# Cutting the first load of w2 in two, and moving the gate's sum between the halves

## The chip, the cores and the metric

The kernel runs on one core of a Trainium2 chip. The metric is the time of one execution on the device in microseconds (us). A second source is the hardware profile of one execution, with the start and length of every instruction. All data is float32.

## The reference

The reference is one decode step of a transformer block for 4 sequences with one token each (model width 512): an attention over the last 2048 entries of a key/value cache with 32 query and 8 key/value heads, and a gated MLP with inner width 1792. Both are conditioned by a vector c: silu(c) times w_mod gives six vectors per sequence, a shift, a scale and a gate for each half.

```python
mod = (_silu(c) @ w_mod).reshape(c.shape[0], 6, 1, -1)
sa, ca, ga, sb, cb, gb = (mod[:, 0], ..., mod[:, 5])
h = _layernorm(x) * (1 + ca) + sa
x = x + ga * attention(h)                # wq, 2048 cached keys and values, softmax, wo
h = _layernorm(x) * (1 + cb) + sb
hidden = _silu(h @ w1) * (h @ w3)        # 512 -> 1792
x = x + gb * (hidden @ w2)               # 1792 -> 512
```

The change concerns the last line alone: the product with w2, and the gate gb.

## The kernel before, in words

One instance of everything: there is no outer loop over data, and the instructions of each engine are written out in order. What one engine needs of another is awaited with semaphores. All large loads are issued by SyncE (SP) through the helper `load` at line 89, on one queue and in the order in which they are used: the conditioning weights, then keys, values and attention weights for the eight head groups, then w_mod's middle part, w1 and w3, the gate's part of w_mod (`gb_in`, 1 MB), and last w2. A load goes out when the buffer it overwrites is free; the last ten or so are all issued long before their data is used, and from then on they follow one another on the queue.

TensorE works through the attention in a loop over pairs of head groups (block "pair"), and then goes on in the straight code of block "post". Matrix products go through the helper `mm` (line 266), transposes through `turn` (line 287). The batch has only 4 rows, so a product here has 4 columns of weights loaded, and four products that write to partitions 0, 32, 64 and 96 of the same PSUM tile are placed side by side.

The end of block "post", which the change touches, goes like this:

- `hidT` is the hidden vector, transposed, in 14 chunks of 128 (lines 424 to 440; line 440 writes the last of it). w2 has 1792 rows, so 14 chunks of 128 rows by 512 columns, 256 KB each. `CHUNKS` is the order in which they are loaded and used.
- The gate: four products of silu(c) with the gate's weights go to the four quarters of tile `bM` (line 445). ScalarE copies them to `gb_sb` (448). A product with `same`, a matrix of zeros and ones, adds the four quarters and lays the sum out as four blocks of 128 columns at partitions 0, 32, 64 and 96 of tile `bT` (line 462); ScalarE copies that to `gbJ` (465). This is "the gate's sum".
- w2's first `HEAD` = 8 chunks: chunk n multiplies its 512 columns into quarter n % 4 of tile `bO` (line 456). VectorE copies `bO` to `y_sb` (459), and four products with `same` add the four quarters into tile `bX`, in the same layout as the gate's sum (475). This is "the sum of y".
- The last 6 chunks go into `bX` directly, each in four column blocks of 128 (line 471), so nothing needs to be summed behind them.
- VectorE multiplies `bX` by `gbJ` (478) and adds the residual `x1J` (480), and SP stores the result (482).

`W2_CUTS` says how w2's 14 chunks are cut into loads. Each load has its own semaphore, `dw[i]`, on which TensorE waits before it multiplies that piece.

Of the kernel before, what the change touches and what calls it, by code (L numbers as in the profile page):

```python
# [10 lines left out]
B, D, HQ, G, SK, DH, W, FF = 4, 512, 32, 8, 8192, 128, 2048, 1792  # L11
P = 128
# [2 lines left out]
EPS = 1e-5  # L15
CHUNKS = [(j, c) for c in range(4) for j in range(4) if c < 2 or j < 3]
HEAD = 8
W2_CUTS = [0, 8, 10, 12, 13, 14]
PAIRS = G // 2


# [22 lines left out]
def block_kernel(nc, x_in, t0_in, t1_in, kv_in, w_in, wm_in, f1_in, f2_in, gb_in, w2_in, out):  # L44
    T, v, s, gp, S = nc.tensor, nc.vector, nc.scalar, nc.gpsimd, nc.sync

    def sems(names):
        return [nc.alloc_semaphore(n) for n in names.split()]

    def sb(name, cols, rows=P):  # L50
        return nc.alloc_sbuf_tensor(name, (rows, cols), F32).ap()

    def bank(name):
        return nc.alloc_psum_tensor(name, (P, 512), F32).ap()

    (first,) = sems("first")
    A = Queue(nc, s, "act")
    V = Queue(nc, v, "dve")
    L = Queue(nc, gp, "pool")
    dx, dt0, dt1, dkv, dk, dva, dvb, dwo, dm, df1, df2a, df2b, dgb = sems("dx dt0 dt1 dkv dk dva dvb dwo dm df1 df2a df2b dgb")  # L60
    dw = sems(" ".join(f"dw{i}" for i in range(len(W2_CUTS) - 1)))
    z_ok, q_ok, p_ok, k_ok, va_ok, vb_ok, pt_ok, o_ok, ot_ok = sems("z_ok q_ok p_ok k_ok va_ok vb_ok pt_ok o_ok ot_ok")
    s_done, q_done, qt_done, pp_done, o_done, x_done, a_done, pe, last = sems("s_done q_done qt_done pp_done o_done x_done a_done pe last")
# [6 lines left out]
    ident, same, eps = sb("ident", P), sb("same", B), sb("eps", 1)  # L70
# [3 lines left out]
    q_sb, p_sb, o_sb, a_sb, y_sb, g_sb, u_sb, gb_sb = [sb(n, 512) for n in "q_sb p_sb o_sb a_sb y_sb g_sb u_sb gb_sb".split()]  # L74
# [7 lines left out]
    x1J, gbJ, yt, y = [sb(n, P) for n in "x1J gbJ yt y".split()]  # L82
    zero = y_sb

    bS, bQ, bT, bP, bO, bX, bA, bM = [bank(n) for n in "bS bQ bT bP bO bX bA bM".split()]


    def load(dst, src, sem):
        S.dma_start(dst, src).then_inc(sem, 16)  # L89
# [33 lines left out]
    load(KV[1][:, 6144:8192], gb_in, dgb)  # L123
    for a, b, sem in zip(W2_CUTS[:-1], W2_CUTS[1:], dw):
        load(KV[1][:, 8192 + a * 512 : 8192 + b * 512], w2_in[:, a * 512 : b * 512], sem)
# [139 lines left out]
    def mm(o, lhsT, rhs, start=True, stop=True):  # L265
        return T.matmul(o, lhsT, rhs, start=start, stop=stop, skip_group_check=True)  # L266
# [46 lines left out]
    for k in range(4):  # L313
        for i in range(2):
            ins = mm(bM[32 * i : 32 * i + B, :], sc[:, k * B : (k + 1) * B], T0[:, 16 + (2 * k + i) * 512 : 16 + (2 * k + i + 1) * 512], k == 0, k == 3)
    ins.then_inc(pe, 1)
    T.wait_ge(V.sem, t_h[1])
    for k in range(4):
        ins = T.transpose(bT[:, k * B : (k + 1) * B], h[:, k * P : (k + 1) * P], ident[:B, :B])
# [51 lines left out]
    for k in range(4):  # L371
        for i in range(3):
            at = (3 * k + i) * 512
            ins = mm(bX[32 * i : 32 * i + B, :], sc[:, k * B : (k + 1) * B], KV[0][:, at : at + 512], k == 0, k == 3)
# [19 lines left out]
    for k in range(4):  # L394
        ins = T.transpose(bT[:, k * B : (k + 1) * B], h[:, k * P : (k + 1) * P], ident[:B, :B])
# [4 lines left out]
    def view(t_):  # L400
        return t_.rearrange("p (c j i) -> p c j i", c=4, j=4)
# [4 lines left out]
    for k in range(4):  # L406
        for j in range(4):
            at = 6144 + k * 2048 + j * 512
            ins = mm(bQ[32 * j : 32 * j + B, :], h2T[:, k * B : (k + 1) * B], KV[0][:, at : at + 512], k == 0, k == 3)
# [3 lines left out]
    for k in range(4):  # L413
# [5 lines left out]
        for j in range(3):  # L419
            at = k * 1536 + j * 512  # L420
            ins = mm(bA[32 * j : 32 * j + B, :], h2T[:, k * B : (k + 1) * B], KV[1][:, at : at + 512], k == 0, k == 3)
# [14 lines left out]
    for c in range(4):  # L436
        ins = T.transpose(bS[:, c * P : c * P + 96], u_sb[:96, c * P : (c + 1) * P], ident[:96, :96])
# [6 lines left out]
    for k in range(4):  # L444
        ins = mm(bM[32 * k : 32 * k + B, :], sc[:, k * B : (k + 1) * B], KV[1][:, 6144 + 512 * k : 6144 + 512 * (k + 1)])
    ins.then_inc(pe, 1)
    A.wait((pe, 10))
    t_gb = A.op(s.copy(gb_sb, bM))
    T.wait_ge(V.sem, t_hid[1])
    hw = view(hidT)  # L450
    w2 = KV[1][:, 8192 : 8192 + 14 * 512].rearrange("p (n m) -> p n m", n=14)
    T.wait_ge(dw[0], 16)
    for n in range(HEAD):
        j, c = CHUNKS[n]
        i = n % 4
        ins = mm(bO[32 * i : 32 * i + B, :], hw[:, c, j, :], w2[:, n, :], n < 4, n >= HEAD - 4)
    ins.then_inc(pe, 1)
    V.wait((pe, 11))
    t_y = V.op(v.tensor_copy(y_sb, bO))
    T.wait_ge(A.sem, t_gb[1])  # L460
    for j in range(4):
        ins = mm(bT[32 * j : 32 * j + B, :P], same, gb_sb[:, j * P : (j + 1) * P])
    ins.then_inc(pe, 1)
    A.wait((pe, 12))
    t_gb = A.op(s.copy(gbJ, bT[:, :P]))
    for i in range(1, len(W2_CUTS) - 1):
        T.wait_ge(dw[i], 16)
        for n in range(W2_CUTS[i], W2_CUTS[i + 1]):
            jj, c = CHUNKS[n]
            for j in range(4):  # L470
                ins = mm(bX[32 * j : 32 * j + B, :P], hw[:, c, jj, :], w2[:, n, j * P : (j + 1) * P], n == HEAD, n == 13)
        if i == 1:
            T.wait_ge(V.sem, t_y[1])
            for j in range(4):
                mm(bX[32 * j : 32 * j + B, :P], same, y_sb[:, j * P : (j + 1) * P], False, False)
# [56 lines left out]
```

## Time and profile before

| | us |
|---|---|
| median of 3 runs | 244.55 |
| lowest and highest of them | 243.27, 245.59 |
| the profiled execution | 245.33 |
| its span, first to last instruction | 244.0 |
| DMA queue of SP, share of the span in which its packets moved | 96.9% |
| TensorE busy, share of the span | 57% |
| mean granted clock of TensorE | 0.811 |

How to read the profile: times are us from the start of the span. PE is TensorE, PEld its weight loads, DVE VectorE, ACT ScalarE, SP SyncE. An instruction is named by its line, the tile it writes and the tiles it reads (`bO<-KV,hidT`); the buffers `KV0` and `KV1` are both called KV. Each `mm` shows as two instructions on PE. The granted clock is 1.00 where TensorE runs at full speed and 0.50 where it runs at half. For a load, "to landing" counts from its issue to the moment when its data is complete; loads of w2 are listed as `KV<-w_in`, with the other loads by the names of their sources. A view in windows gives, for each stretch of time, the busy time of each engine with the count of instructions.

### The profile page before, as it was taken

How to read it: one execution, taken by the hardware profiler on the slowest of the kernel's cores; microseconds unless marked ns; L12 is line 12 of the kernel's file. 1: busy time of each engine (PE TensorE's matmuls, PEld its weight loads, DVE VectorE, ACT ScalarE, POOL GpSimd, SP SyncE). 2: the span in 40 equal slices, each digit the busy share in tenths (PEclk: the TensorE clock that was granted, in tenths of full speed). 3: DMA queues.
4: the chain of work that ended last, by engine and by line, in shares of the span. 5: the costliest groups of instructions: out<-in, count | busy, mean ns of one | idle time of the engine just before them, and what ended most of it. 6: DMA issues, size and time to landing. Idle time of an engine off the chain costs nothing. (4 is left out here: it accounts for less than half of the span.)

```text
span 244.0 us, 2237 instructions
## 1 busy us (share of the span) xinstructions
PE 138.5 (57%) x940; PEld 39.2 (16%) x940; DVE 38.6 (16%) x126; ACT 25.2 (10%) x54; POOL 1.7 (1%) x14
## 2 busy tenths in 40 slices
PE   3451047826771477278615763696057758728756
PEld 0010001301220112012101220121012221202203
DVE  6020002202200022022000320220004022150202
ACT  4010001101010021001100210002002111060100
POOL 2000000000000000000000000000000000000000
PEclk9995557988798589767975996779659988997967
DMA  7998999989898989898989898989899999999980
GB/s 255 430 521 346 505 430 430 451 387 500 381 494 365 505 365 496 355 505 365 494 365 494 365 494 355 505 365 494 379 432 446 418 416 434 445 397 426 434 352 16
DMA packets 3901, 101.34 MB, mean 415 GB/s; under 512 B 436, under 2 KB 564, under 8 KB 1080
## 3 DMA queue, kind: packets, MB, share of 16 engines
q1 hardware_dynamic: 3888, 101.26, 96.9%
q8 instruction: 3, 0.05, 0.1%
q10 hardware_dynamic: 8, 0.01, 0.0%
q14 instruction: 2, 0.02, 0.0%
HBM read 101.20 MB, written 0.07 MB: 415 GB/s over the span
## 5 line engine op out<-in xcount | busy, mean ns | idle before, releaser
L266 PE MATMUL bS<-KV,Z 128*16 128x512 f32 x256 | 44.4, 857 | 53.1 <-PEq L269 53.1
L266 PE MATMUL bO<-KV,pT 128*16 128x512 f32 x256 | 31.0, 626 | 0.5
L266 PEld LDWEIGHTS bS<-KV,Z 128*16 128x16 f32 x256 | 9.5, 126 | 82.3 <-issue 82.3
L222 DVE TENSOR_REDUCE MX<-bS 128x1 f32<-128x512 f32 x8 | 5.5, 692 | 95.9 <-PE bS L266 95.9
L230 ACT ACTIVATE p_sb<-bS,NB 128x512 f32<-128x512 f32 x8 | 5.5, 687 | 116.6 <-DVE NB L228 116.6
L287 PE MATMUL bP<-ident,p_sb 128*128 128x128 f32 x32 | 6.2, 329 | 16.6 <-PEq L269 16.6
L266 PE MATMUL bA<-WP,oT 128*4 128x512 f32 x64 | 11.7, 811 | 3.1 <-PEq L269 3.1
L266 PEld LDWEIGHTS bO<-KV,pT 128*16 128x16 f32 x256 | 8.0, 105 | 23.2 <-issue 23.2
L251 ACT ACTIVATE o_sb<-bO,LB 128x512 f32<-128x512 f32 x8 | 5.5, 687 | 47.3 <-PE bO L266 47.3
L287 PE MATMUL bX<-ident,o_sb 128*128 128x128 f32 x32 | 5.0, 280 | 7.2 <-PEq L269 7.2
L266 PE MATMUL bM<-KV,sc 128*4 128x512 f32 x24 | 6.0, 713 | 4.8 <-DVE sc L188 4.8
L266 PE MATMUL bQ<-WP,hT 128*4 128x512 f32 x64 | 8.3, 592 | 0.6 <-DVE hT L197 0.6
L254 DVE TENSOR_REDUCE oT<-bX 128x16 f32<-128x64 f32 x8 | 1.8, 225 | 41.4 <-PE bX L287 41.4
L287 PEld LDWEIGHTS bP<-ident,p_sb 128*128 128x128 f32 x32 | 4.1, 164 | 24.0 <-issue 24.0
L287 PE MATMUL bT<-ident,q_sb 128*128 128x128 f32 x32 | 5.3, 292 | 3.2 <-PEq L269 3.2
L201 ACT ACTIVATE q_sb<-bQ 128x512 f32<-128x512 f32 x8 | 4.7, 593 | 12.5 <-PE bQ L266 12.5
L287 PEld LDWEIGHTS bX<-ident,o_sb 128*128 128x128 f32 x32 | 3.4, 142 | 14.3 <-issue 14.3
L235 DVE COPY pT<-bP 128x256 f32<-128x256 f32 x8 | 3.4, 425 | 14.2 <-PE bP L287 14.2
L266 PE MATMUL bQ<-KV,h2T 128*4 128x512 f32 x32 | 5.1, 799 | 0.3 <-DVE h2T L398 0.3
L266 PE MATMUL bO<-KV,hidT 128*4 128x512 f32 x16 | 3.6, 1047 | 2.7 <-DMA KV<-w_in 2.7
L287 PEld LDWEIGHTS bT<-ident,q_sb 128*128 128x128 f32 x32 | 3.5, 144 | 7.1 <-issue 6.8
L266 PE MATMUL bX<-KV,sc 128*4 128x512 f32 x24 | 4.1, 592 | 0.0
(100 smaller groups left out, 65.4 us busy)
## 6 DMA issues: line engine op xcount, KB each, us to landing
WP<-w_in SPq DMA_DIRECT2D x3, 4096.0 KB, 21.9
KV<-kv_in SPq DMA_DIRECT2D x1, 4096.0 KB, 24.6
KV<-f_in SPq DMA_DIRECT2D x1, 4096.0 KB, 28.1
KV<-kv_in SPq DMA_DIRECT2D x1, 3072.0 KB, 31.4
KV<-wm_in SPq DMA_DIRECT2D x1, 3072.0 KB, 18.7
KV<-f_in SPq DMA_DIRECT2D x2, 1536.0 KB, 19.1
KV<-t_in SPq DMA_DIRECT2D x1, 2056.0 KB, 7.7
WP<-t_in SPq DMA_DIRECT2D x1, 2048.0 KB, 12.2
```

Source lines behind the costliest of these rows:

```text
L201: A.op(s.mul(q_sb, bQ, DH**-0.5), q_ok)
L222: t = V.op(v.reduce_max(MX[:, 0:1], bS, axis=AX.X))
L230: A.op(s.activation(p_sb, bS, AF.Exp, bias=NB[:, 0:1], accum_out=SM[:, 0:1]), p_ok)
L235: v.tensor_copy(pT.rearrange("p (t b c r) -> p c b t r", t=NT, b=B, c=4), bP.rearrange("p (c b i) -> p c b i", c=4, b=B)[:, :, :, :16].rea ...
L251: A.op(s.mul(o_sb, bO, LB[:, 0:1]), o_ok)
L254: V.op(v.tensor_reduce(oT.rearrange("p (r b) -> p r b", r=R), diag, axis=AX.X, op=ALU.add), ot_ok)
L266: return T.matmul(o, lhsT, rhs, start=start, stop=stop, skip_group_check=True)
L287: ins = T.transpose(dst[:, c * P : (c + 1) * P], src[:, c * P : (c + 1) * P], ident)
```

## The change

w2 is cut into six loads in place of five: 4, 4, 2, 2, 1 and 1 chunks, where before the first 8 came as one. The 8 chunks' products stay what they are, but the first four wait for the first load alone, the second four for the second. The gate's sum, which stood behind all eight, stands between the fours. The copy of `bO`, the sum of y and the last six chunks keep their order; the semaphore that counts TensorE's steps now counts the gate's sum as the 11th and the eight products as the 12th.

```diff
-W2_CUTS = [0, 8, 10, 12, 13, 14]
+W2_CUTS = [0, 4, 8, 10, 12, 13, 14]
...
-    T.wait_ge(dw[0], 16)
-    for n in range(HEAD):
-        j, c = CHUNKS[n]
-        i = n % 4
-        ins = mm(bO[32 * i : 32 * i + B, :], hw[:, c, j, :], w2[:, n, :], n < 4, n >= HEAD - 4)
-    ins.then_inc(pe, 1)
-    V.wait((pe, 11))
-    t_y = V.op(v.tensor_copy(y_sb, bO))
-    T.wait_ge(A.sem, t_gb[1])
-    for j in range(4):
-        ins = mm(bT[32 * j : 32 * j + B, :P], same, gb_sb[:, j * P : (j + 1) * P])
-    ins.then_inc(pe, 1)
-    A.wait((pe, 12))
-    t_gb = A.op(s.copy(gbJ, bT[:, :P]))
-    for i in range(1, len(W2_CUTS) - 1):
+    for i in range(len(W2_CUTS) - 1):
         T.wait_ge(dw[i], 16)
         for n in range(W2_CUTS[i], W2_CUTS[i + 1]):
             jj, c = CHUNKS[n]
+            if n < HEAD:
+                ins = mm(bO[32 * (n % 4) : 32 * (n % 4) + B, :], hw[:, c, jj, :], w2[:, n, :], n < 4, n >= HEAD - 4)
+                continue
             for j in range(4):
                 ins = mm(bX[32 * j : 32 * j + B, :P], hw[:, c, jj, :], w2[:, n, j * P : (j + 1) * P], n == HEAD, n == 13)
+        if i == 0:
+            T.wait_ge(A.sem, t_gb[1])
+            for j in range(4):
+                ins = mm(bT[32 * j : 32 * j + B, :P], same, gb_sb[:, j * P : (j + 1) * P])
+            ins.then_inc(pe, 1)
+            A.wait((pe, 11))
+            t_gb = A.op(s.copy(gbJ, bT[:, :P]))
         if i == 1:
+            ins.then_inc(pe, 1)
+            V.wait((pe, 12))
+            t_y = V.op(v.tensor_copy(y_sb, bO))
+        if i == 2:
             T.wait_ge(V.sem, t_y[1])
             for j in range(4):
                 mm(bX[32 * j : 32 * j + B, :P], same, y_sb[:, j * P : (j + 1) * P], False, False)
```

On TensorE, near the end of block "post", before (-) and now (+); `bM` is the gate's products, `bT` the gate's sum, `bO` the first eight chunks, `bX` the result, and `dw0` to `dw5` are the loads' semaphores:

```order
 L266 MATMUL bM<-KV,sc 4x512 x3
 L266 MATMUL bO<-KV,hidT 4x512 [waits dw0,dve]
-L266 MATMUL bO<-KV,hidT 4x512 x7
+L266 MATMUL bO<-KV,hidT 4x512 x3
 L266 MATMUL bT<-gb_sb,same 4x128 [waits act]
 L266 MATMUL bT<-gb_sb,same 4x128 x3
-L266 MATMUL bX<-KV,hidT 4x128 [waits dw1]
+L266 MATMUL bO<-KV,hidT 4x512 [waits dw1]
+L266 MATMUL bO<-KV,hidT 4x512 x3
+L266 MATMUL bX<-KV,hidT 4x128 [waits dw2]
 L266 MATMUL bX<-KV,hidT 4x128 x7
 L266 MATMUL bX<-y_sb,same 4x128 [waits dve]
```

Four of the eight products into `bO` moved behind the gate's sum and wait for a semaphore of their own, and each later piece's semaphore has a number one higher.

On SP, the loads at the end of its queue (`w_in` is w2; 128x4096 are 8 chunks):

```order
 L89 DMA KV<-f_in 128x3072 x2
 L89 DMA KV<-gb_in 128x2048
-L89 DMA KV<-w_in 128x4096
+L89 DMA KV<-w_in 128x2048 x2
 L89 DMA KV<-w_in 128x1024 x2
 L89 DMA KV<-w_in 128x512 x2
```

The one load of 8 chunks became two of 4 with half the row length each; the four behind it are the same, one place later.

## The prediction

> **What bounds the kernel now.** I read the profile from its end. The chain of waits comes first (start, length, what):
>
> ```profile
> core 0 of [0], span 244.0 us
> ...
> 208.07 27.21 DMA KV<-w_in
> 235.28 0.14 issue
> 235.41 3.59 PE bO L266 x16
> 239.01 0.43 PE bT L266 x8
> 239.43 2.32 PE bX L266 x56
> 241.76 0.02 issue
> 241.78 0.30 DVE yt L478
> 242.08 0.02 issue
> 242.11 0.29 DVE y L480
> ```
>
> The kernel waits for the first piece of w2 (8 chunks) until 235.28, and from then on TensorE works without a pause until 241.76: 6.35 us of work behind one landing. Two short additions and the store follow. So two things can end the kernel, the stream of loads and that burst of work, and the question is which is later once the burst may start earlier. For the stream I took the load instruction's line in narrow windows, which give each transfer's issue and its time to landing:
>
> ```profile
> L89 SPq DMA_DIRECT2D KV<-gb_in x1: 444/444/444, 207.6 to 207.6; - x1
> L89 SPq DMA_DIRECT2D KV<-w_in x1: 431/431/431, 208.1 to 208.1; - x1
> DMA to landing us min/median/max: 22.8/25.0/27.2
> ...
> L89 SPq DMA_DIRECT2D KV<-w_in x2: 432/432/432, 208.5 to 209.0; - x2
> DMA to landing us min/median/max: 28.0/28.4/28.8
> ...
> L89 SPq DMA_DIRECT2D KV<-w_in x2: 433/2758/5084, 209.5 to 210.0; - x2
> DMA to landing us min/median/max: 29.0/29.0/29.1
> ```
>
> Issue plus time to landing gives the landings: the gate's weights 207.6 + 22.8 = 230.4; w2's 8 chunks 235.3; its two pieces of two chunks 208.5 + 28.0 = 236.5 and 209.0 + 28.8 = 237.8; its two single chunks 209.5 + 29.0 = 238.5 and 210.0 + 29.1 = 239.1. The whole stream has landed at 239.1, and TensorE ends 2.7 us behind it. That 2.7 us, less what the last chunk needs in any case, is all that an order of work can save.
>
> Next, why that work takes so long: the line of the products in windows of 3.41 us (busy time and count on TensorE and its weight loads, granted clock, share of the DMA engines, GB/s), and the products of the two tiles (durations min/median/max in ns):
>
> ```profile
> 186.21:189.63 3.42, 1.22 (x12) 0.42 (x16) 1.00 1.07 460
> 189.63:193.04 3.41, 2.41 (x24) 0.53 (x16) 1.00 0.89 382
> 196.45:199.87 3.42, 1.21 (x12) 0.13 (x4) 1.00 0.90 383
> 199.87:203.28 3.41, 2.12 (x12) 0.45 (x16) 0.50 1.11 471
> 206.69:210.11 3.42, 1.04 (x8) 0.14 (x8) 1.00 1.15 491
> 210.11:213.52 3.41, 3.06 (x22) 0.87 (x25) 1.00 0.98 418
> 230.59:234.00 3.41, 1.04 (x8) 0.11 (x8) 1.00 0.95 400
> 234.00:237.41 3.41, 2.00 (x12) 0.45 (x16) 0.50 0.95 366
> 237.41:240.83 3.42, 3.42 (x48) 1.67 (x44) 0.50 0.06 22
> 240.90:241.80 0.90, 0.81 (x32) 0.47 (x20) 1.00 0.00 0
> ...
> L266 PE MATMUL bO<-KV,hidT x16: 1012/1057/1061, 235.4 to 237.9; 128*4 128x512 f32 x16
> ...
> L266 PE MATMUL bX<-KV,hidT x48: 272/300/421, 239.2 to 241.4; 128*4 128x128 f32 x48
> ```
>
> The clock is half from 234.00 to about 240.83, nearly the whole burst. In this trace it changes only at the borders of such windows: it falls at the end of a window with few products (1.21 us at 199.87, 1.04 us at 234.00) and is kept after 1.22 us at 189.63. After 1.04 us at 210.11 it was kept too, so between 1.04 and 1.21 us it went both ways; I count on nothing below 1.22. TensorE stood idle ahead of the late piece, and that idle time then made the work slow as well.
>
> **The change part by part.** Prices and the other early steps, from the timeline (start, length, engine):
>
> ```profile
> 231.69 1.04 PE L266 MATMUL bM<-KV,sc 128*4 128x512 f32 x8
> 231.80 0.20 DVE L440 TENSOR_TENSOR hidT<-sT,bS 128x48 f32<-128x48 f32 x1 [0.64 <-PE bS L437]
> 232.80 0.59 ACT L448 COPY gb_sb<-bM 128x512 f32<-128x512 f32 x1 [3.95 <-PE bM L266]
> 239.07 0.69 DVE L459 COPY y_sb<-bO 128x512 f32<-128x512 f32 x1 [7.07 <-PE bO L266]
> 240.06 0.66 PE L266 MATMUL bX<-y_sb,same 128*4 128x128 f32 x8
> 242.43 0.35 SPq L482 DMA_DIRECT2D out<-y  x1
> ```
>
> Each product shows as two instructions, so four chunks are 8 instructions of 128x512, as in the row of the gate's products: 1.04 us at full clock. At half clock 16 took 3.59 us with 1.06 us for the last alone; that is three steps of four, (3.59 - 1.06) / 3 = 0.84 us each, so 8 take 0.84 + 1.06 = 1.90 us.
>
> *The first piece is halved.* The first four chunks lie first in the stream. The 8 chunks came 4.9 us after the gate's weights (230.4 to 235.3), so half of them at the same pace lands at about 232.8. That is an estimate. Its lower bound is 230.4, when the gate's weights are complete; its upper bound is 235.3, if rows of half the length came at half the pace. The gate's own weights have the shorter row and the full pace, so I take 232.8. The gate's products end at 231.69 + 1.04 = 232.73 and hidT is ready at 232.00, so TensorE goes on almost at once: 0.14 us from landing to start, as in the chain, puts the start at 232.95 and the end at 234.0.
>
> *The gate's sum between the fours.* Its operand gb_sb is ready at 232.80 + 0.59 = 233.39, ahead of 234.0, so the moved wait holds nothing up. The four small products took 0.43 us at half clock by the chain; at full clock that is about 0.22, ending near 234.25. Behind them in TensorE's order is only the second four, whose data isn't there before 235.3. So 0.43 us of the old burst goes under a wait, with 1.0 us of cover; ScalarE's copy of the sum follows it, and only the last multiplication reads that. VectorE's copy of y keeps its place in its queue.
>
> *The second four.* They land when the 8 chunks did, at 235.3, start at 235.41 and end at 236.45 at full clock. The copy of y takes 0.69 us: 236.5 to 237.2.
>
> *The rest at full clock.* A chunk cut in four column blocks is 8 instructions of 128x128, priced like the gate's sum: 0.22 us. Chunks 8 and 9 land at 236.5 and take 0.43, to 237.1. The sum of y waits for its copy and ends by 237.7. Chunks 10 and 11 land at 237.8 and are done at 238.4, chunk 12 lands at 238.5 and is done at 238.9, chunk 13 lands at 239.1. Every piece is finished before the next lands. The end is then the last landing 239.1, plus 0.14 to start, plus 0.11 (half of the 0.22, until the second group of four starts), plus 0.27 for the last instruction (the minimum of its row): 239.62. At half clock these two terms are 0.21 and 0.42: 239.87.
>
> *The clock.* The gap of 235.41 - 232.73 = 2.68 us shrinks to 0.2 us and one of 235.41 - 234.25 = 1.16 us. In the window to 234.00 the first four add about 1.0 us to the 1.04 us that stood there: some 2.0 us, and the clock is kept by the rows above. I moved the window along the forecast: the poorest place, about 234.25 to 237.66, still holds 1.04 + 0.43 + 0.21 = 1.7 us, above the 1.22 us that kept it. [...]
>
> *One more load on SP's queue.* It adds one issue of 0.43 us near 208.5 and moves the four behind it by as much; the last of them already took 5.08 us (the largest of its row), to about 215.1. A second such wait would reach about 220, still far ahead of 235, so it costs nothing on the path. Completing one more transfer is the unknown. From below it is nothing: the last two single chunks land 238.5 and 239.1, 0.6 us apart, which is the pace of the stream alone (4.9 us / 8 = 0.61 a chunk). From above it is a whole small transfer by itself, the store:
>
> ```profile
> out<-y SPq DMA_DIRECT2D x1, 64.0 KB, 1.5
> ```
>
> I take nothing, since the last chunks are the nearer row: same queue, same kind, others ahead. [...]
>
> *Sum.* VectorE's start moves from 241.78 to 239.65: 2.13 us saved. The profiled execution took 245.33 us, its span of 244.0 and 1.33 around it: 245.33 - 2.13 = **243.2**. It lies 0.78 above the median of 244.55; the fastest of the three is 243.27. I read that spread as tails that were slow for different lengths, which no row here shows of the other two; then, against the median the saving is only 1.35 us (0.55%).
>
> **The rivals.**
>
> - *The clock falls all the same* (0.12), with a border in the new gap of 1.16 us and half clock to the end. For it: 1.04 us lost the clock, and the new windows are only worked out. Against it: 1.7 us is well above 1.22. Second four 235.41 to 237.3, TensorE free for the next at 237.1; chunks 8 and 9 (0.86) to 238.0; copy of y to 238.05, and by the rows above 0.3 us from copy to product, 238.35 to 238.8; chunks 10 to 13 at 0.43 each to 240.5, and 0.2 for the last to end: 240.7. That saves 1.1 and gives 244.2.
> - *The median's distance is the stream's, not the tail's* (0.14): all three runs had the profile's slow tail, and the loads came earlier in two of them. Then all 2.13 us comes off the median: 242.4. For it: nothing shown says why the three runs differ. Against it: the fastest run stands almost exactly on the landing-bound time.
> - *The new landing costs its own completion* (0.10), the case on the other side: slower than the median of before. At the border between the two fours the stream pays up to the store's 1.5 us, and every later landing moves with it; the end is bound by the last landing, so it shows in full: 243.2 + 1.5 = 244.7, 0.15 above the median. It decides from 1.35 us on. Against it are the five close landings; for it, that pieces of this length were not split here before.
> - *The cut does not bring the first four early* (0.04), landing with the rest at 235.3. Then only the gate's sum can go below, behind a wait it now shares, and the end stays at the profile's: about 244.5.
>
> **How the numbers follow.** The forecast, a landing-bound end with the clock kept, has 0.60 and its own range of 242.7 to 243.8 (0.25 for a slow last chunk, the rest for the estimated landings). The range of 242.2 to 244.7 takes in the half-clock case, most of the stream's case and the lower half of the costly landing; about 2 in 10 is outside. This kernel's measurement can tell about 1% (2.4 us) from no change. Faster by over 1% means below 242.1, which needs the stream's case with some luck: 0.12. Slower by over 1% means above 247.0, more than any case prices: 0.03. Within 1%: 0.85.
>
> **What would show it.** In the profile of the changed kernel: the first piece's landing about 2.4 us ahead of the second's; the first 8 instructions of bO near 233 in about 1.04 us; the gate's sum inside the wait for the second piece; a clock of 1.00 over 234 to 237; TensorE waiting for w_in ahead of each later piece; and the chain ending in the last landing near 239.1, with VectorE's multiplication 0.5 us behind it. The prediction is wrong if the last landing itself moves by more than 0.5 us, if the clock is 0.50 while the second four run, or if bX is still working off pieces long landed when it ends.

## The result and the profile after

| | before | after |
|---|---|---|
| median, us (20 runs each) | 244.63 | 243.34 |
| lowest and highest, us | 243.27, 245.80 | 243.01, 243.49 |
| the profiled execution, us | 245.33 | 243.49 |
| its span, us | 244.0 | 242.2 |

The ratio of the times is 0.9949, with a 95% interval of 0.9931 to 0.9967: about 0.5% faster, 1.3 us in the median. The spread shrank as well. The 20 times of before form two groups with nothing between them, 7 at 243.27 to 243.50 and 13 at 244.43 to 245.80; the 20 times after lie where the lower group does.

The chain of waits after (start, length, what):

```profile
215.35 24.07 DMA KV<-w_in
239.42 0.04 issue
239.46 0.45 PE bX L266 x8
239.91 0.02 issue
239.93 0.30 DVE yt L478
240.23 0.02 issue
240.25 0.29 DVE y L480
```

Where 6.35 us of TensorE's work stood behind the first landing, 0.45 us now stand behind the last one. VectorE's multiplication starts at 239.93 instead of 241.78, 1.85 us earlier, and the span is 1.8 us shorter. TensorE's part of the same stretch, with VectorE's copy of y, in the timeline:

```profile
232.65 1.04 PE L266 MATMUL bM<-KV,sc 128*4 128x512 f32 x8
233.51 1.04 PE L266 MATMUL bO<-KV,hidT 128*4 128x512 f32 x8
234.40 0.40 PE L266 MATMUL bT<-gb_sb,same 128*4 128x128 f32 x8
235.66 1.04 PE L266 MATMUL bO<-KV,hidT 128*4 128x512 f32 x8 [0.86 <-DMA KV<-w_in]
236.77 0.69 DVE L471 COPY y_sb<-bO 128x512 f32<-128x512 f32 x1 [3.81 <-PE bO L266]
236.94 0.62 PE L266 MATMUL bX<-KV,hidT 128*4 128x128 f32 x16 [0.24 <-DMA KV<-w_in]
237.51 0.40 PE L266 MATMUL bX<-y_sb,same 128*4 128x128 f32 x8
238.18 1.05 PE L266 MATMUL bX<-KV,hidT 128*4 128x128 f32 x24 [0.27 <-DMA KV<-w_in]
239.46 0.40 PE L266 MATMUL bX<-KV,hidT 128*4 128x128 f32 x8 [0.23 <-DMA KV<-w_in]
```

Ahead of four of the five later pieces the products now show a wait for the load, of 0.2 to 0.9 us, and the eight chunks take 1.04 us twice instead of 3.59 us. The products' line in windows (busy time and count on TensorE and its weight loads, granted clock, share of the DMA engines, GB/s):

```profile
229.14:232.55 3.41, 1.89 (x12) 0.30 (x12) 1.00 1.01 423
232.55:235.97 3.42, 2.46 (x28) 0.57 (x32) 1.00 1.00 405
235.97:239.38 3.41, 2.73 (x56) 0.87 (x48) 1.00 0.46 171
...
239.00:240.00 1.00, 0.63 (x16) 0.11 (x8) 1.00 0.00 0
```

The clock stays at 1.00 from 229.14 to the last product. The load line gives the landings (issue, then time to landing):

```profile
L89 SPq DMA_DIRECT2D KV<-gb_in x1: 432/432/432, 208.4 to 208.4; - x1
L89 SPq DMA_DIRECT2D KV<-w_in x1: 432/432/432, 208.9 to 208.9; - x1
DMA to landing us min/median/max: 22.2/23.3/24.3
...
L89 SPq DMA_DIRECT2D KV<-w_in x2: 432/432/432, 208.9 to 209.3; - x2
DMA to landing us min/median/max: 24.3/25.3/26.3
```

The gate's weights land at 208.4 + 22.2 = 230.6, the first four chunks at 208.9 + 24.3 = 233.2 and the second four at 209.3 + 26.3 = 235.6. So the half piece is there 2.4 us ahead of the other.

### The profile page after: what moved, and what is told of

Same layout as the page of the kernel before. It is cut to its first block, busy times and chain, and to the rows that moved or that the text cites. A ratio compares the mean times of both kernels' runs of the same rounds, so it can differ in the third digit from the quotient of the medians.

```text
span 242.2 us, 2238 instructions
## 1 busy us (share of the span) xinstructions
PE 137.2 (57%) x940; PEld 38.1 (16%) x940; DVE 38.6 (16%) x126; ACT 25.2 (10%) x54; POOL 1.7 (1%) x14
## 5 line engine op out<-in xcount | busy, mean ns | idle before, releaser
L266 PE MATMUL bS<-KV,Z 128*16 128x512 f32 x256 | 43.8, 846 | 53.4 <-PEq L269 53.4
L266 PE MATMUL bO<-KV,pT 128*16 128x512 f32 x256 | 32.0, 644 | 0.5
L287 PE MATMUL bP<-ident,p_sb 128*128 128x128 f32 x32 | 5.5, 298 | 16.5 <-PEq L269 16.5
L266 PE MATMUL bA<-WP,oT 128*4 128x512 f32 x64 | 9.8, 683 | 3.9 <-PEq L269 3.7
L266 PE MATMUL bM<-KV,sc 128*4 128x512 f32 x24 | 7.0, 809 | 4.7 <-DVE sc L188 4.7
L266 PE MATMUL bQ<-WP,hT 128*4 128x512 f32 x64 | 9.2, 648 | 0.6 <-DVE hT L197 0.6
L266 PE MATMUL bQ<-KV,h2T 128*4 128x512 f32 x32 | 5.7, 876 | 0.3 <-DVE h2T L398 0.3
L206 DVE TENSOR_REDUCE Z<-bT 128x16 f32<-128x64 f32 x8 | 1.8, 225 | 15.0 <-PE bT L287 14.8
```

What stands on the lines that cost most here:

```text
L206: v.tensor_reduce(Z.rearrange("p (b i) -> p b i", b=B)[:, :, 12 : 12 + R], bT.rearrange("p (r k i) -> p i r k", r=R, k=4)[:, :B], axis=AX. ...
L287: ins = T.transpose(dst[:, c * P : (c + 1) * P], src[:, c * P : (c + 1) * P], ident)
```

## The experiments

The theory: the end is the last landing of the stream as soon as TensorE does not fall behind it, and what made TensorE fall behind was the half clock (0.50 from 234.00 to 240.83) that followed its idle wait of 2.68 us. The rivals: the saving comes from the order of the work alone, whatever the clock; and each landing has a price of its own. Times are medians of 12 runs for each kernel. The first four kernels share 35 runs of the kernel before (median 244.48, 243.00 to 245.74), the last three 29 of them (244.48, 243.11 to 245.85).

### The cut alone

```diff
-        if i == 0:
-            T.wait_ge(A.sem, t_gb[1])
-            for j in range(4):
-                ins = mm(bT[32 * j : 32 * j + B, :P], same, gb_sb[:, j * P : (j + 1) * P])
...
         if i == 1:
             ins.then_inc(pe, 1)
...
             t_y = V.op(v.tensor_copy(y_sb, bO))
+            T.wait_ge(A.sem, t_gb[1])
+            for j in range(4):
+                ins = mm(bT[32 * j : 32 * j + B, :P], same, gb_sb[:, j * P : (j + 1) * P])
...
```

> The first piece is halved as in the change, but the gate's sum stays behind the second four. Theory (the end is the last landing, and the clock is kept): the 0.4 us of the gate's sum lie between the second four and chunks 8 and 9, whose slack to the last landing is about 2 us, so the time stays at the change's 243.3. Rival (the saving comes from moving the gate's sum out of the burst): part of the saving is lost, 243.7 or more.

Measured: 243.35 (243.13 to 243.55), ratio 0.9959 (0.9932 to 0.9985). The gate's sum behind the second four costs nothing. TensorE in its timeline:

```profile
235.32 1.04 PE L266 MATMUL bO<-KV,hidT 128*4 128x512 f32 x8 [1.39 <-DMA KV<-w_in]
236.18 0.40 PE L266 MATMUL bT<-gb_sb,same 128*4 128x128 f32 x8
236.60 0.62 PE L266 MATMUL bX<-KV,hidT 128*4 128x128 f32 x16
237.18 0.40 PE L266 MATMUL bX<-y_sb,same 128*4 128x128 f32 x8
237.88 1.00 PE L266 MATMUL bX<-KV,hidT 128*4 128x128 f32 x24 [0.30 <-DMA KV<-w_in]
```

It uses up the wait ahead of chunks 8 and 9, and TensorE is waiting for loads again at chunk 10. The wait ahead of the second four grows instead, to 1.39 us, and in none of the 12 runs did that bring back the upper group of times. Beside the cut, the move of the gate's sum, half of the edit, is worth nothing that these runs can show.

### The gate's sum alone

```diff
+    T.wait_ge(A.sem, t_gb[1])
+    for j in range(4):
+        ins = mm(bT[32 * j : 32 * j + B, :P], same, gb_sb[:, j * P : (j + 1) * P])
...
     T.wait_ge(dw[0], 16)
     for n in range(HEAD):
...
-    T.wait_ge(A.sem, t_gb[1])
-    for j in range(4):
-        ins = mm(bT[32 * j : 32 * j + B, :P], same, gb_sb[:, j * P : (j + 1) * P])
...
```

> The first piece stays whole (8 chunks), and only the gate's sum moves, to the wait ahead of it. Theory: 0.4 us of products in the old gap leave 1.6 us of idle time and about 1.1 to 1.4 us of products in the window around it, close to the line at which the clock falls. So some executions end at the last landing (243.3) and some at half clock (up to 245), with fewer slow ones than before: a median between 243.3 and 244.3. Rival (only the order of the work counts, not the clock): 0.43 us off every execution of before, so its spread stays and the median is 244.2.

Measured: median 243.38, ratio 0.9975 (0.9945 to 1.0004), so no verdict by the mean. What tells is the distribution: 8 of 12 runs at 243.05 to 243.56 and 4 at 244.44 to 245.19, where before had 11 of 35 in its lower group. Taking 0.43 us off every run would have moved both groups; instead runs changed from one group to the other, as the theory has it. With 12 runs that is a hint and not a proof. The profiled execution is one of the upper four (245.19):

```profile
231.90 1.04 PE L266 MATMUL bM<-KV,sc 128*4 128x512 f32 x8
233.74 0.54 PE L266 MATMUL bT<-gb_sb,same 128*4 128x128 f32 x8 [0.80 <-ACT gb_sb L448]
235.53 3.59 PE L266 MATMUL bO<-KV,hidT 128*4 128x512 f32 x16 [1.25 <-DMA KV<-w_in]
```

And in windows that end at the borders of its clock:

```profile
230.46:233.87 3.41, 1.33 (x18) 0.25 (x16) 1.00 0.95 402
233.87:237.28 3.41, 2.16 (x20) 0.34 (x16) 0.50 0.98 379
237.28:240.69 3.41, 3.41 (x44) 1.21 (x40) 0.50 0.08 31
```

The clock falls at 233.87 with the gate's sum just begun, and the same 3.59 us burst as before follows at half clock.

These rows count the products of line 266 alone, and so do the rows that the prediction used. The transposes (lines 287 and 437) are TensorE's work as well. With them, two windows of the kernel before, after which the clock was kept (the first) and fell (the second), and the window of this run after which it fell (TensorE's busy time and count, granted clock, share of the DMA engines, GB/s):

```profile
206.69:210.11 3.42, 1.67 (x12) 1.00 1.15 491
230.59:234.00 3.41, 1.52 (x12) 1.00 0.95 400
230.46:233.87 3.41, 1.81 (x22) 1.00 0.95 402
```

### Filling the wait, with nothing split or moved

```diff
+    for _ in range(2):
+        for k in range(4):
+            mm(bQ[32 * k : 32 * k + B, :], sc[:, k * B : (k + 1) * B], KV[1][:, 6144 + 512 * k : 6144 + 512 * (k + 1)])
     T.wait_ge(dw[0], 16)
     for n in range(HEAD):
```

> The kernel before, with 16 instructions of 128x512 into an unused tile (the gate's products again, twice, their result unused) in the wait for the 8 chunks; nothing is split or moved. Theory: the clock is kept, the same burst then takes about half as long and ends with the last landing: 243.3 in every execution, spread under 0.6 us, though 1.7 us of work is added. Rival (the work behind the late landing must start earlier): no gain, 244.6 and the old spread.

Measured: 243.24 (243.12 to 243.41), ratio 0.9949 (0.9926 to 0.9973), with all 12 runs in the lower group. This is the run that settles the clock's part. The kernel does 1.7 us more work, all eight chunks still wait for the one late landing, the gate's sum is still behind them, and the gain is that of the change. TensorE's timeline shows why:

```profile
233.63 1.90 PE L266 MATMUL bQ<-KV,sc 128*4 128x512 f32 x16
235.48 1.90 PE L266 MATMUL bO<-KV,hidT 128*4 128x512 f32 x16
237.20 0.40 PE L266 MATMUL bT<-gb_sb,same 128*4 128x128 f32 x8
237.42 0.62 PE L266 MATMUL bX<-KV,hidT 128*4 128x128 f32 x16
238.20 0.40 PE L266 MATMUL bX<-y_sb,same 128*4 128x128 f32 x8 [0.16 <-DVE y_sb L462]
238.41 1.25 PE L266 MATMUL bX<-KV,hidT 128*4 128x128 f32 x32
```

The eight chunks take 1.90 us instead of 3.59, and TensorE has caught up with the last landing by the end. The clock is at 1.00 from 233.00 to 239.00 (busy time and count of TensorE, its weight loads, VectorE, ScalarE and GpSimd, then as above):

```profile
233.00:236.00 3.00, 3.00 (x32) 0.62 (x28) 0.09 (x1) 0.58 (x1) 0.00 (x0) 1.00 0.97 390
236.00:239.00 3.00, 2.84 (x72) 1.52 (x64) 0.69 (x1) 0.27 (x1) 0.00 (x0) 1.00 0.50 184
```

It is close, though: TensorE ends at 239.7 without waiting for the last pieces, so here the work is just about as late as the landing.

### A load for each chunk

```diff
-W2_CUTS = [0, 4, 8, 10, 12, 13, 14]
+W2_CUTS = list(range(15))
```

The gate's sum, the copy of y and the sum of y stay behind the same chunks as in the change.

> The change with w2 in 14 loads of one chunk in place of 6; the order of the work is the same. Theory (a load more costs nothing on the stream): the last landing stays, 243.3, at most 0.3 us more. Rival (each landing costs its own completion): 8 more landings at 0.1 us give 244.1, at the store's 1.5 us 255.

Measured: 243.92 (243.63 to 244.13), ratio 0.9989 (0.9961 to 1.0016). That is 0.57 us above the cut alone, which ran on the same chip, for 8 loads more: 0.07 us each. That is more than the 0.3 us that the theory allowed. So here a load more did have a price, near the 0.1 us that the rival supposed and far from its 1.5 us. The chain of waits:

```profile
230.41 9.45 DMA KV<-w_in
239.86 0.04 issue
239.91 0.45 PE bX L266 x8
```

Behind the last landing all is as after the change; the landing itself is later, at 239.86 instead of 239.42. The last of the 14 loads goes out at 230.41 only: SP's issues of them start at 206.69 and take 24.25 us together, where the 6 of the change take 11.15 us, and two of them, at 223.16 and 225.92, took 2.72 and 1.65 us. Whether the 0.57 us comes from the landings or from these late issues was not told apart.

### One load less

```diff
     for a, b, sem in zip(W2_CUTS[:-1], W2_CUTS[1:], dw):
-        load(KV[1][:, 8192 + a * 512 : 8192 + b * 512], w2_in[:, a * 512 : b * 512], sem)
+        if a < 13:
+            load(KV[1][:, 8192 + a * 512 : 8192 + b * 512], w2_in[:, a * 512 : b * 512], sem)
...
-        T.wait_ge(dw[i], 16)
+        if i < 5:
+            T.wait_ge(dw[i], 16)
...
-                ins = mm(bX[32 * j : 32 * j + B, :P], hw[:, c, jj, :], w2[:, n, j * P : (j + 1) * P], n == HEAD, n == 13)
+                ins = mm(bX[32 * j : 32 * j + B, :P], hw[:, c, jj, :], w2[:, min(n, 12), j * P : (j + 1) * P], n == HEAD, n == 13)
```

> The change without the load of chunk 13: its products multiply chunk 12's data, so the result is not the reference's; TensorE does the same work and waits for five landings. Theory (the end is the last landing): it ends behind the landing of chunk 12, one chunk of the stream earlier (0.6 us), plus 0.22 us for the last chunk's products behind it: 243.3 - 0.6 + 0.2 = 242.9. Rival (TensorE's work sets the end): unchanged, 243.3.

Measured: 242.87 (242.74 to 243.41), ratio 0.9954 (0.9934 to 0.9974), 0.47 us below the change and 0.55 below the next kernel, which ran on the same chip. TensorE's instructions are the same in number and size, so in the change it is the landing of the stream's last 256 KB that sets the end. Without it the two are about even: in the profile chunks 10 and 11 land at 237.88, and from 237.93 to 239.21 TensorE works through chunks 10 to 13 without a wait.

### More work behind the second four

```diff
+        if i == 2:
+            for k in range(4):
+                mm(bQ[32 * k : 32 * k + B, :], sc[:, k * B : (k + 1) * B], KV[1][:, 6144 + 512 * k : 6144 + 512 * (k + 1)])
         T.wait_ge(dw[i], 16)
```

> The change with 8 more instructions of 128x512 into an unused tile (the gate's products once more, result unused) between the second four and chunks 8 and 9. Theory: their 0.86 us fit into TensorE's waits ahead of the later pieces, so the time stays at 243.3, at most 0.1 more. Rival (what lies behind the second four's landing counts in full): 244.2.

Measured: 243.42 (243.26 to 243.73), 0.08 above the change's own median, and ratio 0.9971 (0.9950 to 0.9993). The 0.86 us of extra work vanish in the waits:

```profile
236.45 1.04 PE L266 MATMUL bQ<-KV,sc 128*4 128x512 f32 x8
237.31 0.62 PE L266 MATMUL bX<-KV,hidT 128*4 128x128 f32 x16
237.74 0.40 PE L266 MATMUL bX<-y_sb,same 128*4 128x128 f32 x8
238.11 1.04 PE L266 MATMUL bX<-KV,hidT 128*4 128x128 f32 x24
239.38 0.40 PE L266 MATMUL bX<-KV,hidT 128*4 128x128 f32 x8 [0.23 <-DMA KV<-w_in]
```

TensorE comes to chunk 8 some 0.4 us later than in the profile of the change and waits for the last chunk as it did without the extra work.

### The last loads cut by partitions

An attempt at a faster kernel: with the end on the last landing, an earlier end of the stream would count in full.

```diff
-        load(KV[1][:, 8192 + a * 512 : 8192 + b * 512], w2_in[:, a * 512 : b * 512], sem)
+        for r0, r1 in ((0, P),) if b - a > 1 else ((0, 120), (120, P)):
+            load(KV[1][r0:r1, 8192 + a * 512 : 8192 + b * 512], w2_in[r0:r1, a * 512 : b * 512], sem)
...
-        T.wait_ge(dw[i], 16)
+        T.wait_ge(dw[i], 16 if i < 4 else 32)
```

> The change with chunks 12 and 13 each loaded as 120 partitions and 8 partitions in two loads on one semaphore, to spread the last partitions' share differently over the stream's end. In the profile the traffic thins out from 237 us on while the last landing is at 239.4, so a few slow shares end the stream. If the last 8 partitions are among them, the last landing comes up to 0.6 us earlier: 242.8. If not, two loads more cost 0.07 us each, the price of the 14 pieces: 243.5.

Measured: 244.62 (244.03 to 245.26), ratio 1.0021 (0.9994 to 1.0048): the whole gain is lost, against both cases of the expectation, and it is 1.2 us above the kernel with more work, which ran on the same chip. The timeline shows what became late:

```profile
237.14 0.40 PE L267 MATMUL bX<-y_sb,same 128*4 128x128 f32 x8
239.18 1.89 PE L267 MATMUL bX<-KV,hidT 128*4 128x128 f32 x32 [1.64 <-DMA KV<-w_in]
```

And the products' line in windows to the border of the clock:

```profile
235.67:239.08 3.41, 1.48 (x32) 0.45 (x24) 1.00 0.79 195
239.08:242.49 3.41, 1.89 (x32) 1.02 (x32) 0.50 0.03 11
```

Already chunks 10 and 11, whose load was not changed, were complete only at 239.1, while the change had them by 238.2. TensorE waited 1.64 us for them, the clock fell at 239.08 in that wait, and the products of chunks 10 to 13 took 1.89 us at half clock without a further wait; the same 32 instructions took 1.25 us at full clock in the filled wait. So a late load cost its lateness and the clock as well, the pattern of the kernel before. Why the unchanged load ahead of those of 120 and of 8 partitions landed later was not settled.

## Why the prediction was right

The forecast of 243.2 stands against 243.34. It was worked out from one profiled execution, of 245.33 us; the profiled one after took 243.49, the longest of the 20, so 1.84 us were saved where 2.13 were forecast, and part of the nearness to the median is luck. By its own steps:

- *The first piece is halved; the second four.* The first four landed at 233.2 and the second four at 235.6, against 232.8 and 235.3. The distance between them is 2.4 us, as worked out. In the profiled execution the gate's products ended 0.96 us later than in that of before (233.69 against 232.73), so the first four came behind TensorE's own work and not behind their landing. The cover took that up: TensorE still waited 0.86 us for the second four.
- *The gate's sum.* The step priced it rightly at full clock (about 0.2 us of TensorE's time), but the cut alone shows that it needed no cover: behind the second four it is as free.
- *The rest at full clock.* The forecast had every piece finished before the next lands and the end at the last landing, 239.1, plus 0.52. The last landing was 239.42 and VectorE started 0.51 us behind it. The 0.3 us in the landings are why the profiled saving was 1.85 us and not 2.13.
- *The clock.* It stayed at full over the end of the one execution profiled, and none of the 20 times lies near the 244.2 that half clock was priced at. But the argument for it doesn't hold. Its rows count the products alone; with the transposes, TensorE was busy for 2.33 us in the window of 1.22 us that was taken as the line, and for 1.67 us in the one of 1.04 us that kept the clock. The clock fell after 1.81 us in the run with the gate's sum alone and after 1.48 us in the run with 120 partitions. The 1.7 us of the poorest place forecast lies among these, so it gave no margin, and that the step came out right is in part luck. TensorE's busy time in these windows does not by itself decide; what does stays open.
- *One more load.* Taken at nothing. The run with 14 loads puts it at 0.07 us, a twentieth of the bound taken from the store.
- *The spread of before.* The reading that slow tails of different lengths make it was a guess from three times. The 20 times in two groups, and the filled wait that leaves only the lower one, support it: with nothing split, the median came down by 1.24 us. No profile of a run of before in its lower group was seen, so its full clock there is inferred. The mean clock on record for each run covers the whole span and doesn't tell: it is 0.809 to 0.824 in the lower group of the 64 runs beside the experiments and 0.804 to 0.832 in the upper. That the clock's borders lie elsewhere in another execution the traces do show: the clock first falls 19.0 us from the start in the profile of before, 17.6 us in that of after and 17.2 us in the run with 120 partitions, three kernels that are alike up to the tail. That the border's place decides the group is not shown. The rival that the stream made the spread (242.4) falls with this. The first four landed 2.4 us early and a load more cost 0.07 us, so the other two fall as well.

So the saving is almost wholly the clock's: with the clock kept, the run with the filled wait reaches the same time without the cut and without the move. What the cut brings in order, work that starts 2.4 us earlier, matters only because it keeps TensorE from a long wait (0.86 us in the profile after, 2.68 us before).

## What to carry to other kernels

Here a wait in front of a burst of products cost twice, once as the wait of 2.68 us and once as a burst at half clock, 3.59 us for eight chunks that took 1.90 us in the run with the filled wait; look at the granted clock in windows before reading a burst's length as work. Where a stream of loads runs to the end, compute its last landing plus the work that must follow it: that was the floor here (239.42, and 0.51 us to VectorE's start). Here two cheap ways to keep TensorE going reached it: an earlier piece, and products whose result nobody reads. Two groups of times with a gap between them, here 243.27 to 243.50 and 244.43 to 245.80, are a hint to such a switch, and the number of runs in each group says more there than the median.

## What was not expected of the hardware

- Loads of 120 and 8 partitions in place of 128, for the last 512 KB alone, came with a landing of the unchanged load ahead of them at 239.1 instead of 238.2, and with 1.3 us more in the median (244.62 against 243.34).
- Issuing 14 loads instead of 6 kept SP's queue issuing until after 230.41, 24.25 us for the 14; with 6 in the change it was 11.15 us, of which the last two took 4.55 and 4.66 us, and all were out by 220.
- With the transposes counted, TensorE was busy for 1.48, 1.52 and 1.81 us in windows after which the clock fell, and for 1.67 us in one after which it was kept, so no single line of that number separates the two.
